# Finishing attention heads in pairs, with the softmax division moved behind the transpose, in a cached decode kernel

## The chip, the cores and the metric

The kernel runs on one core of one Trainium2 chip. The metric is the device time of one execution in microseconds (us). The engines are named PE (matmul), PEld (its weight loads), DVE (vector), ACT (scalar), POOL (GpSimd) and SP, which only issues loads here.

## The reference, cut to what matters

Two attention blocks A and B of the same shape are computed and their outputs put side by side. The batch is 2, with 32 heads of 192 in each block, one query, 8192 cached keys and values, and a model width of 640.

```python
q = (x @ wq).reshape(B, 1, 32, 192)
scores = einsum("bhqd,bhkd->bhqk", q, k_cache) * 192 ** -0.5
o = einsum("bhqk,bhkd->bhqd", softmax(scores), v_cache)
out = o.reshape(B, 1, 32 * 192) @ wo              # once for A, once for B
```

## The kernel before

One **unit** is one head of one batch row, so there are 128 units. A unit loads 3 MB of K and 3 MB of V (the cached keys and values), all issued by SP. Each engine's work is put by hand into a table of slots, and the engines then run their tables in order, held only by semaphores. The steps of unit `u` are:

1. DVE multiplies K by the query in two products. `d1a` takes the first `NA` of the 64 key columns, which ACT then sums. `d1b` takes the others, which DVE sums itself. The end of `d1b` frees the K buffer.
2. DVE takes the maximum (`d3`), and POOL reduces it over the partitions (`ar`). ACT takes the exponential, and POOL reduces its sum (`ls`).
3. PE forms P·V with 32 matmuls (`pv`), whose end frees the V buffer.
4. Per head (two units), ACT copies the result out of PSUM, where the matmuls accumulate (`f1`), and DVE forms the reciprocal of the sums (`f2`). PE transposes the result by a matmul against the reciprocals, which also divides (`f3`), ACT copies the transposed result (`f4`), and PE multiplies by `wo` (`f5`).

The tiles stand in memory in the order in which they are made. `ND_MAX` is what the two products' split leaves to DVE, and it sets the size of `prodD`:

```python
NA_MAX = max(NA_MAIN, NA_LAST)                     # 28 and 23: NA of all units, and of the last one
ND_MAX = T - min(NA_MAIN, NA_LAST)                 # 64 - 23 = 41
kb = [sb(f"kb{i}", [128, T, Dh], BF16) for i in range(NK)]
vb = [sb(f"vb{i}", [128, T, Dh], BF16) for i in range(NV)]
prodA = [sb(f"prodA{i}", [128, NA_MAX, Dh], BF16) for i in range(2)]
prodD = sb("prodD", [128, ND_MAX, Dh], BF16)
# ... sc, mp, mg, nb, pb, rs, qbc
wqs = [sb(f"wqs{i}", [128, DC, HG * Dh], BF16) for i in range(2)]
wos = [sb(f"wos{i}", [128, HG // 2, 3, D], BF16) for i in range(2)]
```

The parts of the schedule that the argument touches are these (`put(table, slot, order, work, waits, signal)`):

```python
put(dve_tab, u + 1, 0, dve_d3(u), [("acc", u), ("r", u), key("ar", u - 2)], ("d3", u))
put(dve_tab, u, 2, dve_d1a(u), [("k", u), ("a0", qg_of(u)), key("acc", u - 2)], ("d1a", u))
put(dve_tab, u, 3, dve_d1b(u), ...)
# ...
early = (g == TAILG)                               # TAILG = G - 2, the next-to-last head
put(dve_tab, u1 + 2, 1 if early else 8, dve_f2(g), [("ls", u1), key("f3", g - 2)], ("f2", g))
```

Of the kernel before, what the change touches and what calls it, by code (L numbers as in the profile page):

```python
# [51 lines left out]
def build_kernel(nc, blocks, out, cfg=None):  # L52
# [11 lines left out]
    scale = float(Dh) ** -0.5  # L64

    NA_MAIN = min(cfg.get("NA", 28), T - 2)
    NA_LAST = min(cfg.get("NA_LAST", 23), T - 2)
    WARM = cfg.get("WARM", 3)
    NK = cfg.get("NK", 2)
    NV = cfg.get("NV", 2)  # L70
    HG = cfg.get("HG", 4)
# [24 lines left out]
    with ExitStack() as es:  # L96
# [16 lines left out]
        wos = [sb(f"wos{i}", [128, HG // 2, 3, D], BF16) for i in range(2)]  # L113
        xT = [[sb(f"xT{k}_{b}", [128, DC], BF16) for b in range(B)] for k in range(NBLK)]
        xbc = [[sb(f"xbc{k}_{b}", [128, DC, 128], BF16) for b in range(B)] for k in range(NBLK)]
        o_sb = sb("o_sb", [33, 2, Dh], F32)
        lall = [sb(f"lall{i}", [128, 2], F32) for i in range(2)]
        rc = [sb(f"rc{i}", [33, 2], F32) for i in range(2)]
        oTz = sb("oTz", [128, 3, 6], BF16)
        out_sb = [sb(f"out_sb{k}", [4, NH2], BF16) for k in range(NBLK)]  # L120
        actd = sb("actd", [128, 2], F32)

        qps = ps("qps", [128, 512], F32)
        ops = ps("ops", [128, 2, 512], F32)
        oTps = ps("oTps", [128, 512], F32)
        outps = ps("outps", [128, 512], F32)

# [19 lines left out]
        def key(name, *idx):  # L147
            for i in idx:
                if i < 0:
                    return None  # L150
            return (name,) + tuple(idx)
# [52 lines left out]
        def sp_wo(w):  # L204
            blk = (w * HG) // Hn
            h0 = (w * HG) % Hn
            src = blocks[blk]["wo"][h0 * Dh:(h0 + HG) * Dh, :].rearrange("(pr p i) n -> p pr (i n)", p=128, i=3)
            return dma(wos[w % 2][:].rearrange("p pr i n -> p pr (i n)"), src, wosem[w % 2])
# [50 lines left out]
            return lambda eng: eng.tensor_reduce(sc[u % 2][:, na:T], prodD[:, 0:T - na, 0:24], AXL.X, ALU.add)  # L259

        def dve_f2(g):
            return lambda eng: eng.reciprocal(rc[g % 2][:], lall[g % 2][0:33, :])

        def act_acc(u, t):
            return lambda eng: eng.activation(prodA[u % 2][:, t, :], prodA[u % 2][:, t, :], ACTF.Identity,  # L265
# [6 lines left out]
            return lambda eng: eng.activation(pb[u % 2][:, :, ::32], sc[u % 2][:].rearrange("p (j a) -> p j a", a=2),  # L272
                                              ACTF.Exp, bias=nb[u % 2][:], scale=scale, accum_out=rs[u % 2][:])

        def act_f1(eng):
            eng.activation(o_sb[0:1, :, :], ops[0:1, :, 0:Dh], ACTF.Identity)  # L276
            return eng.activation(o_sb[32:33, :, :], ops[32:33, :, Dh:2 * Dh], ACTF.Identity)  # L277

        def act_f1b(b):
            def fn(eng):  # L280
                eng.activation(o_sb[0:1, b, :], ops[0:1, b, 0:Dh], ACTF.Identity)
                return eng.activation(o_sb[32:33, b, :], ops[32:33, b, Dh:2 * Dh], ACTF.Identity)
            return fn

        def pe_warm(n, uu):
            vw = vb[uu % NV][:].rearrange("p (j a) d -> p j (a d)", a=2)

            def fn(eng):
                for i in range(n):
                    ins = eng.matmul(dps[0:33, 0:QW], pb[uu % 2][:, i % (T // 2), :], vw[:, i % (T // 2), :],  # L290
                                     start=(i == 0), stop=(i == n - 1))
                return ins
            return fn

        def act_f4(g):
            s0 = 64 * (g % 2)
            return lambda eng: eng.activation(oTz[s0:s0 + 64, :, 2:4],
                                              oTps[s0:s0 + 64, 0:6].rearrange("p (i b) -> p i b", i=3), ACTF.Identity)

        def act_a0(qg):  # L300
            return lambda eng: eng.activation(qbc[qg % 4][:], qps[:, 0:QW].rearrange("p (a d) -> p a d", a=2),  # L301
# [2 lines left out]
        def act_out(blk):  # L304
            return lambda eng: eng.activation(out_sb[blk][:], outps[0:4, 0:NH2], ACTF.Identity)  # L305
# [22 lines left out]
        def pe_pv(u, j0, j1):  # L328
            b = u % B
            vv = vb[u % NV][:].rearrange("p (j a) d -> p j (a d)", a=2)  # L330

            def fn(eng):
                for j in range(j0, j1):
                    ins = eng.matmul(ops[0:33, b, 0:QW], pb[u % 2][:, j, :], vv[:, j, :],  # L334
                                     start=(j == 0), stop=(j == T // 2 - 1))
                return ins
            return fn

        def pe_f3(g):
            s0 = 64 * (g % 2)  # L340

            def fn(eng):
                for i in range(3):
                    for b in range(B):
                        ins = eng.matmul(oTps[s0:s0 + 64, 2 * i + b:2 * i + b + 1],  # L345
                                         o_sb[:, b, :].rearrange("p (r i) -> p i r", i=3)[:, i, :],
                                         rc[g % 2][:, b:b + 1], start=True, stop=True)
                return ins
            return fn

        def pe_f5(g):
            first = (g % Hn == 0)
            last = (g % Hn == Hn - 1)
            w = g // HG
            pr = (g % HG) // 2
            s0 = 64 * (g % 2)

            def fn(eng):
                for i in range(3):
                    for half in range(2):  # L360
                        ins = eng.matmul(outps[0:4, 0:NH2], oTz[s0:s0 + 64, i, 2 - 2 * half:6 - 2 * half],  # L361
                                         wos[w % 2][s0:s0 + 64, pr, i, half * NH2:(half + 1) * NH2],
                                         start=(first and i == 0 and half == 0),
                                         stop=(last and i == 2 and half == 1))
                return ins
            return fn

        NSLOT = NU + 8
        TAILG = G - 2 if G >= 3 else -1

        dve_tab = [[] for _ in range(NSLOT)]
        act_tab = [[] for _ in range(NSLOT)]
# [3 lines left out]
        def put(tab, slot, order, fn, waits, sig):  # L376
            tab[slot].append((order, len(tab[slot]), fn, waits, sig))

        for u in range(NU):
# [14 lines left out]
                w = [("d1a", u), key("d3", u - 2), key("exp", u - 2)] if t == 0 else []  # L394
                put(act_tab, u, 10 + t, act_acc(u, t), w, ("acc", u) if t == na_of(u) - 1 else None)
            pc = pieces(u)
            w0 = [("exp", u), key("f1", g - 1), ("init",)]
            if pc is None:
                put(pe_tab, u, 0, pe_pv(u, 0, T // 2), w0 + [("v", u)], ("pv", u))
            else:  # L400
                for i, (t0, t1, sm) in enumerate(pc):
                    put(pe_tab, u, 0, pe_pv(u, t0 // 2, t1 // 2), (w0 if i == 0 else []) + [("vp", u, i)],
                        ("pv", u) if i == len(pc) - 1 else None)

        for g in range(G):
            u1 = 2 * g + 1
            early = (g == TAILG)
            if g == G - 1 and G >= 3:
                put(act_tab, u1 + 1, 3, act_f1b(0), [("pv", u1 - 1), key("f3", g - 1), ("init",)], ("f1a", g))
                put(act_tab, u1 + 2, 2, act_f1b(1), [("pv", u1), ("f1a", g)], ("f1", g))  # L410
            else:
                put(act_tab, u1 + 2, 2, act_f1, [("pv", u1), key("f3", g - 1), ("init",)], ("f1", g))
            put(dve_tab, u1 + 2, 1 if early else 8, dve_f2(g), [("ls", u1), key("f3", g - 2)], ("f2", g))
            put(pe_tab, u1 + 1 if early else u1 + 2, 3 if early else 1, pe_f3(g),
                [("f2", g), ("f1", g), key("f4", g - 1)], ("f3", g))
            put(act_tab, u1 + 3 if early else u1 + 4, 2 if early else 3, act_f4(g),
                [("f3", g), key("f5", g - 2), ("init",)], ("f4", g))
            w = [("f4", g), ("wo", g // HG)]
            if g % Hn == 0 and g > 0:
                w.append(("oev", g // Hn - 1))  # L420
            put(pe_tab, u1 + 3, 2, pe_f5(g), w, ("f5", g))
            if g == G - 1 and G >= 3 and WARM:
                put(pe_tab, u1 + 2, 1.5, pe_warm(WARM, NU - 1), [], ("warm", 1))
            if g % Hn == Hn - 1:
                blk = g // Hn
                put(act_tab, u1 + 5, 95, act_out(blk), [("f5", g)], ("oev", blk))
                put(act_tab, u1 + 5, 96, act_out_dma(blk, 0), [("oev", blk)], None)
                put(act_tab, u1 + 5, 97, act_out_dma(blk, 1), [("oev", blk)], None)

# [25 lines left out]
        for kind, u in korder:  # L455
            if kind == "k":
                if u in KSPLIT:
                    S_sp.add(sp_k(u, 0), waits=[key("d1b", u - NK)])
                    S_sp.add(sp_k(u, 1))
                else:  # L460
                    S_sp.add(sp_k(u), waits=[key("d1b", u - NK)])
                if u == 0:
                    if WQSPLIT:
                        S_sp.add(sp_wq(0, 1))
                    for blk in range(1, NBLK):
                        for b in range(B):
                            S_sp.add(sp_x(blk, b))
                w = u // UG
                if u % UG == 1:
                    S_sp.add(sp_wo(w), waits=[key("f5", (w - 2) * HG + HG - 1)])  # L470
                if u % UG == (3 if UG >= 8 else 0) and w + 1 < NWG:
                    S_sp.add(sp_wq(w + 1), waits=[key("pq", (w - 1) * HG + HG - 1)])
            else:
                add_v(u)

        S_pool.add(lambda eng: eng.memset(o_sb[:], 0.0))
        for i in range(2):
            S_pool.add((lambda i: (lambda eng: eng.memset(pb[i][:], 0.0)))(i))
        S_pool.add(lambda eng: eng.memset(oTz[:], 0.0), sig=("init",))
        for blk in range(1, NBLK):  # L480
            for b in range(B):
                S_pool.add(xbc_copy(blk, b), waits=[("x", blk)], sig=("xbc", blk) if b == B - 1 else None)
# [80 lines left out]
```

## Time and profile before

| | before |
|---|---|
| time, median of 4 runs | 2016.54 us (2011.67 to 2017.82) |
| DMA engines busy with the main queue | 98.6% |
| DVE, ACT, PE busy | 74%, 71%, 57% |
| last whole K load (unit 126) landed | 1971.72 us |
| last V load (unit 127) landed | 2001.81 us |
| end of the span | 2014.77 us |

The page of the kernel before, cut to its head and the parts on slices, queues and the chain of waits. In the second part each position is a fortieth of the span, and the GB/s row gives what the DMA engines moved in it:

```profile
span 2014.8 us, 20972 instructions
PE 1144.6 (57%) x5571; PEld 606.8 (30%) x5571; DVE 1482.1 (74%) x962; ACT 1436.9 (71%) x7805; POOL 113.0 (6%) x266
...
DMA  9999999999999999999999999999999999999995
GB/s 386 428 427 428 430 426 428 428 428 429 426 426 426 423 410 424 418 424 415 423 425 410 428 413 419 430 405 430 414 421 426 408 422 417 420 427 416 425 420 212
...
q1 hardware_dynamic: 55856, 836.79, 98.6%
q8 instruction: 44, 0.72, 0.1%
...
DMA 77%; DVE 21%; PE 1%; ACT 1%; POOL 0%; issue 0%; SPq 0%
```

The loads fill the span. The chain is K loads and the DVE products that free their buffers, and PE, ACT and POOL have next to no part in it. The waits say the same of PE. The columns are who waited, for what, us in total, times and the longest:

```profile
PE ops L334 <- DMA vb<-in_A_v_cache_dram: 442.9, 64, 23.0
PE ops L334 <- DMA vb<-in_B_v_cache_dram: 412.2, 62, 9.8
```

PE waits for V in 126 of 128 units. The chain of waits has no load in it after the K load of unit 126, the last that is loaded whole (unit 127's comes in two parts). From there on compute sets the pace, so this tail is shown closely. Here are DVE and then POOL of the kernel before, in order of time. The columns are start, duration in us, engine, line, operation, tiles, and in brackets the idle time before it and what ended that:

```profile
1984.56 0.22 DVE L251 TENSOR_REDUCE mp<-sc 128x1 f32<-128x64 f32 x1 [1.37 <-ACT prodA L265]
1984.69 0.15 DVE L262 RECIPROCAL rc<-lall 33x2 f32<-33x2 f32 x1
1984.77 2.43 DVE L244 TENSOR_TENSOR prodA<-kb,qbc 128x4416 bf16<-128x4416 bf16 x1
1987.12 4.24 DVE L248 TENSOR_TENSOR prodD<-kb,qbc 128x7872 bf16<-128x7872 bf16 x1
...
1984.87 6.71 POOL L231 PARTITION_ALL_REDUCE mg<-mp  x1 [13.07 <-DVE rc L262]
```

The reduction over partitions needs 0.35 us elsewhere in this trace (0.352 to 0.354 us in the other 127 units). Here it took 6.71 us, until both products were done, and ACT waited 7.09 us for it.

### The profile page before, as it was taken

Reading aid. Unit: us, or ns where it says so; the run is one execution under the profiler, and the core shown is the slowest. Engines: PE = TensorE matmul, PEld = TensorE weight load, DVE = VectorE, ACT = ScalarE, POOL = GpSimd, SP = SyncE. Lnnn points to the kernel's source line nnn. Section 1 sums busy time; section 2 is a strip of 40 time slices with the busy share of each in tenths; the row PEclk is TensorE's granted clock in tenths of the full one; section 3 lists DMA queues with packets and bytes.
Section 4 is the critical chain, followed back from the end, with each engine's and each line's share of the span. In section 5 each row is a group of like instructions: output and inputs, shape, how many; then the busy total and the mean of one; then the engine's idle time right before and its main releaser. Section 6 shows DMA issues by size and latency. Waiting matters only on the chain.

```text
span 2014.8 us, 20972 instructions
## 1 busy us (share of the span) xinstructions
PE 1144.6 (57%) x5571; PEld 606.8 (30%) x5571; DVE 1482.1 (74%) x962; ACT 1436.9 (71%) x7805; POOL 113.0 (6%) x266
## 2 busy tenths in 40 slices
PE   2565556556555565555655566555655565556557
PEld 1232233223232233223322333223322233223323
DVE  7776877867677777777777767777677767877775
ACT  6776777767767676776777767767677776777675
POOL 1000000000000001000000000000000000000001
PEclk9777777777777777777777777777777777777777
DMA  9999999999999999999999999999999999999995
GB/s 386 428 427 428 430 426 428 428 428 429 426 426 426 423 410 424 418 424 415 423 425 410 428 413 419 430 405 430 414 421 426 408 422 417 420 427 416 425 420 212
DMA packets 55991, 838.13 MB, mean 416 GB/s; under 512 B 7352, under 2 KB 18240, under 8 KB 22848
## 3 DMA queue, kind: packets, MB, share of 16 engines
q1 hardware_dynamic: 55856, 836.79, 98.6%
q8 instruction: 44, 0.72, 0.1%
q14 instruction: 75, 0.61, 0.1%
q10 hardware_dynamic: 16, 0.01, 0.0%
HBM read 836.77 MB, written 0.01 MB: 415 GB/s over the span
## 4 chain that ended last, share of the span: by engine, by line
DMA 77%; DVE 21%; PE 1%; ACT 1%; POOL 0%; issue 0%; SPq 0%
DMA kb<-in_B_k_cache_dram 39%; DMA kb<-in_A_k_cache_dram 38%; DVE prodD L248 12%; DVE prodA L244 9%; PE ops L334 1%; ACT prodA L265 0%; POOL mg L231 0%; PE outps L361 0%; PE oTps L345 0%; SPq L184 0%; SPq L191 0%; PE dps L290 0%; ACT o_sb L277 0%; ACT pb L272 0%; ACT out_sb L305 0%
## 5 line engine op out<-in xcount | busy, mean ns | idle before, releaser
L334 PE MATMUL ops<-vb,pb 128*33 128x384 bf16 x4096 | 952.7, 408 | 861.1 <-DMA vb<-in_A_v_cache_dram 442.9
L265 ACT ACTIVATE prodA<-prodA 128x192 bf16<-128x192 bf16 x3579 | 1238.5, 350 | 205.3 <-DVE prodA L244 204.6
L334 PEld LDWEIGHTS ops<-vb,pb 128*33 128x33 bf16 x4096 | 481.8, 120 | 1321.0 <-issue 1171.7
L265 ACT ACTIVATION_READ_ACCUMULATOR prodA<-prodA 128x1 f32 x3579 | 677.4, 189 | 0.0
L244 DVE TENSOR_TENSOR prodA<-kb,qbc 128x5376 bf16<-128x5376 bf16 x128 | 378.2, 2954 | 316.6 <-DMA kb<-in_A_k_cache_dram 160.2
L248 DVE TENSOR_TENSOR prodD<-kb,qbc 128x6912 bf16<-128x6912 bf16 x128 | 480.7, 3756 | 1.2 <-DMA kb<-in_A_k_cache_dram 1.2
L255 DVE TENSOR_TENSOR prodD<-prodD 128x3456 bf16<-128x3456 bf16 (+2 forms) x384 | 465.0, 1211 | 13.3
L251 DVE TENSOR_REDUCE mp<-sc 128x1 f32<-128x64 f32 x128 | 28.2, 220 | 180.0 <-ACT prodA L265 179.9
L231 POOL PARTITION_ALL_REDUCE mg<-mp x128 | 51.4, 402 | 1773.7 <-DVE mp L251 1760.7
L259 DVE TENSOR_REDUCE sc<-prodD 128x36 f32<-128x864 bf16 x128 | 134.9, 1054 | 4.4
L276 ACT ACTIVATE o_sb<-ops 1x384 f32<-1x384 f32 x63 | 30.3, 480 | 129.1 <-PE oTps L345 127.7
L301 ACT ACTIVATE qbc<-qps 128x384 bf16<-128x384 f32 x64 | 31.5, 492 | 125.4 <-PE qps L322 124.6
L269 ACT ACTIVATE nb<-mg 128x1 f32<-128x1 f32 x128 | 26.0, 203 | 100.8 <-POOL mg L231 100.8
L345 PEld LDWEIGHTS oTps<-rc,o_sb 33*64 33x64 f32 x768 | 72.0, 171 | 20.2 <-issue 20.2
L345 PE MATMUL oTps<-rc,o_sb 33*64 33x1 f32 x768 | 77.5, 225 | 0.0
L322 PE MATMUL qps<-wqs,xbc 128*128 128x384 bf16 x320 | 64.7, 334 | 6.7 <-DMA wqs<-in_A_wq_dram 6.1
L361 PE MATMUL outps<-wos,oTz 64*4 64x320 bf16 x384 | 62.3, 296 | 0.0
L235 POOL PARTITION_ALL_REDUCE lall<-rs x128 | 54.9, 429 | 103.0 <-ACT pb L272 103.0
L272 ACT ACTIVATE pb<-sc,nb 128x64 bf16<-128x64 f32 x128 | 52.2, 408 | 4.3
L361 PEld LDWEIGHTS outps<-wos,oTz 64*4 64x4 bf16 x384 | 26.3, 81 | 34.2 <-issue 16.2
L322 PEld LDWEIGHTS qps<-wqs,xbc 128*128 128x128 bf16 x320 | 26.4, 99 | 29.8 <-issue 9.9
L277 ACT ACTIVATE o_sb<-ops 1x384 f32<-1x384 f32 x63 | 30.4, 482 | 0.7
(20 smaller groups left out, 57.5 us busy)
## 6 DMA issues: line engine op xcount, KB each, us to landing
vb<-in_A_v_cache_dram SPq DMA_DIRECT2D x64, 3072.0 KB, 23.0
kb<-in_A_k_cache_dram SPq DMA_DIRECT2D x63, 3072.0 KB, 23.9
kb<-in_B_k_cache_dram SPq DMA_DIRECT2D x63, 3072.0 KB, 23.7
vb<-in_B_v_cache_dram SPq DMA_DIRECT2D x62, 3072.0 KB, 23.3
wos<-in_A_wo_dram SPq DMA_DIRECT2D x8, 960.0 KB, 25.2
wqs<-in_B_wq_dram SPq DMA_DIRECT2D x8, 960.0 KB, 27.9
wos<-in_B_wo_dram SPq DMA_DIRECT2D x8, 960.0 KB, 25.2
wqs<-in_A_wq_dram SPq DMA_DIRECT2D x7, 960.0 KB, 27.8
```

Of the source, the lines that this page charges most:

```text
L231: return lambda eng: eng.partition_all_reduce(mg[u % 2][:], mp[u % 2][:], 128, bass.bass_isa.ReduceOp.max)
L235: return lambda eng: eng.partition_all_reduce(lall[g % 2][:, b:b + 1], rs[u % 2][:], 128, bass.bass_isa.ReduceOp.add)
L244: return lambda eng: eng.tensor_tensor(prodA[u % 2][:, 0:na, :], kb[u % NK][:, 0:na, :], qb_bc(u, na), ALU.mult)
L248: return lambda eng: eng.tensor_tensor(prodD[:, 0:T - na, :], kb[u % NK][:, na:T, :], qb_bc(u, T - na), ALU.mult)
L255: return lambda eng: eng.tensor_tensor(prodD[:, 0:nd, 0:w], prodD[:, 0:nd, 0:w], prodD[:, 0:nd, w:2 * w], ALU.add)
L259: return lambda eng: eng.tensor_reduce(sc[u % 2][:, na:T], prodD[:, 0:T - na, 0:24], AXL.X, ALU.add)
L265: return lambda eng: eng.activation(prodA[u % 2][:, t, :], prodA[u % 2][:, t, :], ACTF.Identity, accum_out=sc[u % 2][:, t:t + 1])
L272: return lambda eng: eng.activation(pb[u % 2][:, :, ::32], sc[u % 2][:].rearrange("p (j a) -> p j a", a=2), ACTF.Exp, bias=nb[u % 2][:], s ...
L322: ins = eng.matmul(qps[:, 0:QW], xbc[blk][b][:, c, :], wqs[w % 2][:, c, off:off + QW], start=(c == 0), stop=(c == DC - 1))
L334: ins = eng.matmul(ops[0:33, b, 0:QW], pb[u % 2][:, j, :], vv[:, j, :], start=(j == 0), stop=(j == T // 2 - 1))
L345: ins = eng.matmul(oTps[s0:s0 + 64, 2 * i + b:2 * i + b + 1], o_sb[:, b, :].rearrange("p (r i) -> p i r", i=3)[:, i, :], rc[g % 2][:, b:b ...
L361: ins = eng.matmul(outps[0:4, 0:NH2], oTz[s0:s0 + 64, i, 2 - 2 * half:6 - 2 * half], wos[w % 2][s0:s0 + 64, pr, i, half * NH2:(half + 1) * ...
```

## The change

Its intent is to do the steps `f3` to `f5` once per head pair at 128 partitions instead of once per head at 64. The division moves out of the transpose into the copy after it, where it is a per-partition scale. A second PSUM accumulator lets the next head's P·V start before the copy. The tail's two constants were tuned anew, and warm-up matmuls on zeros were put before unit 126. The diff, cut to its core:

```diff
-    NA_LAST = min(cfg.get("NA_LAST", 23), T - 2)
-    WARM = cfg.get("WARM", 3)
+    NA_LAST = min(cfg.get("NA_LAST", 26), T - 2)
+    WARM = cfg.get("WARM", 10)
...
-        ops = ps("ops", [128, 2, 512], F32)
+        ops = [ps(f"ops{i}", [128, 2, 512], F32) for i in range(2)]
...
-        def act_f4(g):
-            s0 = 64 * (g % 2)
-            return lambda eng: eng.activation(oTz[s0:s0 + 64, :, 2:4],
-                                              oTps[s0:s0 + 64, 0:6].rearrange("p (i b) -> p i b", i=3), ACTF.Identity)
+        def act_f4(pp):
+            def fn(eng):
+                for b in range(B):
+                    ins = eng.activation(oTz[pp % 2][:, :, 2 + b], oTps[:, b:6:2], ACTF.Identity,
+                                         scale=rcT[pp % 2][:, b:b + 1])
+                return ins
+            return fn
...
+        def pe_f3(eng):
+            for i in range(3):
+                for b in range(B):
+                    ins = eng.matmul(oTps[:, 2 * i + b:2 * i + b + 1],
+                                     o_sb[:, b, :, :].rearrange("p s (r i) -> p i (s r)", i=3)[:, i, :],
+                                     ones33[:], start=True, stop=True)
+            return ins
...
-            w0 = [("exp", u), key("f1", g - 1), ("init",)]
+            w0 = [("exp", u), key("f1", g - 2), ("init",)]
...
-            put(dve_tab, u1 + 2, 1 if early else 8, dve_f2(g), [("ls", u1), key("f3", g - 2)], ("f2", g))
+            put(dve_tab, u1 + 2, 8, dve_f2(g), [("ls", u1), key("f4", pp - 2)], ("f2", g))
...  (f3 to f5 per pair; in the last pair f3 is cut into two halves)
```

More of the change, by code (lines that the diff above doesn't have):

```diff
@@ L115, in build_kernel @@
         xbc = [[sb(f"xbc{k}_{b}", [128, DC, 128], BF16) for b in range(B)] for k in range(NBLK)]
-        o_sb = sb("o_sb", [33, 2, Dh], F32)
+        o_sb = sb("o_sb", [33, 2, 2, Dh], F32)
+        ones33 = sb("ones33", [33, 1], F32)
+        wdl = sb("wdl", [128, 33], BF16)
+        wdr = sb("wdr", [128, QW], BF16)
         lall = [sb(f"lall{i}", [128, 2], F32) for i in range(2)]
-        rc = [sb(f"rc{i}", [33, 2], F32) for i in range(2)]
-        oTz = sb("oTz", [128, 3, 6], BF16)
+        rcT = [sb(f"rcT{i}", [128, 2], F32) for i in range(2)]
+        oTz = [sb(f"oTz{i}", [128, 3, 6], BF16) for i in range(2)]
         out_sb = [sb(f"out_sb{k}", [4, NH2], BF16) for k in range(NBLK)]
@@ L261, in dve_f2 @@
         def dve_f2(g):
-            return lambda eng: eng.reciprocal(rc[g % 2][:], lall[g % 2][0:33, :])
+            s0 = 64 * (g % 2)
+            return lambda eng: eng.reciprocal(rcT[(g // 2) % 2][s0:s0 + 64, :], lall[g % 2][s0:s0 + 64, :])
         def act_acc(u, t):
@@ L273, in act_exp, with act_f1, act_f1b, fn @@
                                               ACTF.Exp, bias=nb[u % 2][:], scale=scale, accum_out=rs[u % 2][:])
-        def act_f1(eng):
-            eng.activation(o_sb[0:1, :, :], ops[0:1, :, 0:Dh], ACTF.Identity)
-            return eng.activation(o_sb[32:33, :, :], ops[32:33, :, Dh:2 * Dh], ACTF.Identity)
-        def act_f1b(b):
+        def act_f1(g):
+            hs = g % 2
             def fn(eng):
-                eng.activation(o_sb[0:1, b, :], ops[0:1, b, 0:Dh], ACTF.Identity)
-                return eng.activation(o_sb[32:33, b, :], ops[32:33, b, Dh:2 * Dh], ACTF.Identity)
+                eng.activation(o_sb[0:1, :, hs, :], ops[hs][0:1, :, 0:Dh], ACTF.Identity)
+                return eng.activation(o_sb[32:33, :, hs, :], ops[hs][32:33, :, Dh:2 * Dh], ACTF.Identity)
+            return fn
+        def act_f1b(g, b):
+            hs = g % 2
+            def fn(eng):
+                eng.activation(o_sb[0:1, b, hs, :], ops[hs][0:1, b, 0:Dh], ACTF.Identity)
+                return eng.activation(o_sb[32:33, b, hs, :], ops[hs][32:33, b, Dh:2 * Dh], ACTF.Identity)
             return fn
         def pe_warm(n, uu):
-            vw = vb[uu % NV][:].rearrange("p (j a) d -> p j (a d)", a=2)
             def fn(eng):
                 for i in range(n):
-                    ins = eng.matmul(dps[0:33, 0:QW], pb[uu % 2][:, i % (T // 2), :], vw[:, i % (T // 2), :],
-                                     start=(i == 0), stop=(i == n - 1))
-                return ins
-            return fn
-        def act_f4(g):
-            s0 = 64 * (g % 2)
-            return lambda eng: eng.activation(oTz[s0:s0 + 64, :, 2:4],
-                                              oTps[s0:s0 + 64, 0:6].rearrange("p (i b) -> p i b", i=3), ACTF.Identity)
+                    ins = eng.matmul(dps[0:33, 0:QW], wdl[:], wdr[:], start=(i == 0), stop=(i == n - 1))
+                return ins
+            return fn
+        def act_f4(pp):
+            def fn(eng):
+                for b in range(B):
+                    ins = eng.activation(oTz[pp % 2][:, :, 2 + b], oTps[:, b:6:2], ACTF.Identity,
+                                         scale=rcT[pp % 2][:, b:b + 1])
+                return ins
+            return fn
         def act_a0(qg):
@@ L333, in fn @@
                 for j in range(j0, j1):
-                    ins = eng.matmul(ops[0:33, b, 0:QW], pb[u % 2][:, j, :], vv[:, j, :],
+                    ins = eng.matmul(ops[(u // B) % 2][0:33, b, 0:QW], pb[u % 2][:, j, :], vv[:, j, :],
                                      start=(j == 0), stop=(j == T // 2 - 1))
@@ L337, in pe_pv, with pe_f3h @@
             return fn
-        def pe_f3(g):
-            s0 = 64 * (g % 2)
+        def pe_f3(eng):
[5 more added lines that the diff above has]
+            return ins
+        def pe_f3h(hs):
+            s0 = 64 * hs
             def fn(eng):
@@ L345, in fn, with pe_f5 @@
                         ins = eng.matmul(oTps[s0:s0 + 64, 2 * i + b:2 * i + b + 1],
-                                         o_sb[:, b, :].rearrange("p (r i) -> p i r", i=3)[:, i, :],
-                                         rc[g % 2][:, b:b + 1], start=True, stop=True)
-                return ins
-            return fn
-        def pe_f5(g):
-            first = (g % Hn == 0)
-            last = (g % Hn == Hn - 1)
-            w = g // HG
-            pr = (g % HG) // 2
-            s0 = 64 * (g % 2)
+                                         o_sb[:, b, hs, :].rearrange("p (r i) -> p i r", i=3)[:, i, :],
+                                         ones33[:], start=True, stop=True)
+                return ins
+            return fn
+        def pe_f5(pp):
+            g0 = 2 * pp
+            first = (g0 % Hn == 0)
+            last = (g0 % Hn == Hn - 2)
+            w = g0 // HG
+            pr = (g0 % HG) // 2
             def fn(eng):
@@ L360, in fn @@
                     for half in range(2):
-                        ins = eng.matmul(outps[0:4, 0:NH2], oTz[s0:s0 + 64, i, 2 - 2 * half:6 - 2 * half],
-                                         wos[w % 2][s0:s0 + 64, pr, i, half * NH2:(half + 1) * NH2],
+                        ins = eng.matmul(outps[0:4, 0:NH2], oTz[pp % 2][:, i, 2 - 2 * half:6 - 2 * half],
+                                         wos[w % 2][:, pr, i, half * NH2:(half + 1) * NH2],
                                          start=(first and i == 0 and half == 0),
@@ L368, in build_kernel @@
         NSLOT = NU + 8
-        TAILG = G - 2 if G >= 3 else -1
         dve_tab = [[] for _ in range(NSLOT)]
@@ L403, in build_kernel @@
                         ("pv", u) if i == len(pc) - 1 else None)
+        LASTP = G // 2 - 1 if G >= 4 else -99
         for g in range(G):
             u1 = 2 * g + 1
-            early = (g == TAILG)
-            if g == G - 1 and G >= 3:
-                put(act_tab, u1 + 1, 3, act_f1b(0), [("pv", u1 - 1), key("f3", g - 1), ("init",)], ("f1a", g))
-                put(act_tab, u1 + 2, 2, act_f1b(1), [("pv", u1), ("f1a", g)], ("f1", g))
-            else:
-                put(act_tab, u1 + 2, 2, act_f1, [("pv", u1), key("f3", g - 1), ("init",)], ("f1", g))
@@ L413, in build_kernel @@
-            put(dve_tab, u1 + 2, 1 if early else 8, dve_f2(g), [("ls", u1), key("f3", g - 2)], ("f2", g))
-            put(pe_tab, u1 + 1 if early else u1 + 2, 3 if early else 1, pe_f3(g),
-                [("f2", g), ("f1", g), key("f4", g - 1)], ("f3", g))
-            put(act_tab, u1 + 3 if early else u1 + 4, 2 if early else 3, act_f4(g),
-                [("f3", g), key("f5", g - 2), ("init",)], ("f4", g))
-            w = [("f4", g), ("wo", g // HG)]
-            if g % Hn == 0 and g > 0:
-                w.append(("oev", g // Hn - 1))
@@ L421, in build_kernel @@
-            put(pe_tab, u1 + 3, 2, pe_f5(g), w, ("f5", g))
-            if g == G - 1 and G >= 3 and WARM:
-                put(pe_tab, u1 + 2, 1.5, pe_warm(WARM, NU - 1), [], ("warm", 1))
-            if g % Hn == Hn - 1:
-                blk = g // Hn
-                put(act_tab, u1 + 5, 95, act_out(blk), [("f5", g)], ("oev", blk))
+            pp = g // 2
+            w1 = [key("f3", pp - 1), ("init",)]
+            if pp == LASTP and g % 2 == 0:
+                put(act_tab, u1 + 3, 2, act_f1(g), [("pv", u1)] + w1, ("f1", g))
+            elif pp == LASTP:
+                put(act_tab, u1 + 1, 3, act_f1b(g, 0), [("pv", u1 - 1)] + w1, ("f1a", g))
+                put(act_tab, u1 + 2, 2, act_f1b(g, 1), [("pv", u1), ("f1a", g)], ("f1", g))
+            else:
+                put(act_tab, u1 + 2, 2, act_f1(g), [("pv", u1)] + w1, ("f1", g))
@@ new lines, in build_kernel @@
+            put(dve_tab, u1 + 2, 8, dve_f2(g), [("ls", u1), key("f4", pp - 2)], ("f2", g))
+        for pp in range(G // 2):
+            g1 = 2 * pp + 1
+            u1 = 2 * g1 + 1
+            if pp == LASTP:
+                put(pe_tab, u1 + 1, 1, pe_f3h(0), [("f1", g1 - 1), key("f4", pp - 1), ("init",)], ("f3a", pp))
+                put(pe_tab, u1 + 2, 1, pe_f3h(1), [("f1", g1), ("f3a", pp)], ("f3", pp))
+            else:
+                put(pe_tab, u1 + 2, 1, pe_f3, [("f1", g1 - 1), ("f1", g1), key("f4", pp - 1), ("init",)], ("f3", pp))
+            put(act_tab, u1 + 5 if pp == LASTP - 1 else u1 + 4, 3.5 if pp == LASTP - 1 else 3, act_f4(pp),
+                [("f3", pp), ("f2", g1 - 1), ("f2", g1), key("f5", pp - 2), ("init",)], ("f4", pp))
+            w = [("f4", pp), ("wo", (2 * pp) // HG), key("f5", pp - 1)]
+            if (2 * pp) % Hn == 0 and pp > 0:
+                w.append(("oev", (2 * pp) // Hn - 1))
+            put(pe_tab, u1 + 6 if pp == LASTP - 1 else u1 + 3, 1.2 if pp == LASTP - 1 else 2, pe_f5(pp), w, ("f5", pp))
+            if pp == LASTP and WARM:
+                put(pe_tab, u1 - 1, -0.5, pe_warm(WARM, NU - 3), [("init",)], ("warm", 1))
+            if g1 % Hn == Hn - 1:
+                blk = g1 // Hn
+                put(act_tab, u1 + 5, 95, act_out(blk), [("f5", pp)], ("oev", blk))
@@ L469, in build_kernel @@
                 if u % UG == 1:
-                    S_sp.add(sp_wo(w), waits=[key("f5", (w - 2) * HG + HG - 1)])
+                    S_sp.add(sp_wo(w), waits=[key("f5", ((w - 2) * HG + HG - 1) // 2 if w >= 2 else -1)])
                 if u % UG == (3 if UG >= 8 else 0) and w + 1 < NWG:
@@ L476, in build_kernel @@
         S_pool.add(lambda eng: eng.memset(o_sb[:], 0.0))
+        S_pool.add(lambda eng: eng.memset(ones33[:], 1.0))
+        S_pool.add(lambda eng: eng.memset(wdl[:], 0.0))
+        S_pool.add(lambda eng: eng.memset(wdr[:], 0.0))
         for i in range(2):
             S_pool.add((lambda i: (lambda eng: eng.memset(pb[i][:], 0.0)))(i))
-        S_pool.add(lambda eng: eng.memset(oTz[:], 0.0), sig=("init",))
+        S_pool.add(lambda eng: eng.memset(oTz[0][:], 0.0))
+        S_pool.add(lambda eng: eng.memset(oTz[1][:], 0.0), sig=("init",))
         for blk in range(1, NBLK):
```

## The prediction

> **What bounds the kernel now.** DMA. The page shows 837 MB in 2014.8 us, the 16 DMA engines 98.6% busy with the main queue; PE is 57%, DVE 74%, ACT 71% busy. The chain of waits is 77% K-cache loads plus 21% DVE products that free the K buffers. PE waits for V loads 126 times (855 us); a load lands a median 23 us after issue, so the queue keeps about 1.5 units (15.5 us each) of backlog.
>
> **One DMA engine is late.** The landing increments of each load (16, one per engine) show 15 engines together and one behind: 0.4 us at the start, 4 us more every 12 units, then a constant 12.5 us with the others held back; the page's GB/s falls from about 428 to 418. The packet list has a PE instruction queue (q8): 44 packets of 16 KB, 1.01 us each, one per 46 us: 2.2%, the same as the lag's growth (4.1 us per 186 us). My reading, an inference: PE's instruction fetch shares that engine, and that engine's work sets the time.[...]
>
> **The loop.** Per head pair instead of per head, transposes (768 matmuls, 77.5 us busy) and output projections (384, 62.3 us) halve; the doubled output accumulator spares the next head's PV the wait for the eviction (about 1 us). All this compute is slack behind DMA, worth about nothing directly. But PE goes from 5571 matmuls to about 5014; with weight loads about 1110 fewer of 11290 instructions, 4 to 5 fetches of 1.01 us: estimate -4.5 us.
>
> **The tail** (last 30 us) is where compute counts:
> - The all-reduce at 1984.9 took 6.7 us rather than 0.35 because DVE products ran back to back. [...]Max-reduce, then product: the order stays, so does the stall.
> - PV 126 no longer waits for the 0.96 us eviction; warm-up matmuls before it may raise its clock (8.3 us cold, 5.4 warm). But the last unit's ACT sums (23 to 26, +1.0 us at 0.345) start about 1 us earlier, so the last exp still ends about 2002.8; PV 127 starts 0.6 us earlier than 2003.5.
> - After it, two half transposes (1.14 us each) in a row and one projection replace projection, transpose, projection: 4.2 us for 3.6.
> - Risk: if PV 126 runs warm, PE idles up to 5 us before PV 127, which may start cold (+2 to +3 us).
> In sum about +0.7 us (0 to +3).
>
> **Prediction:** 2016.5 - 4.5 + 0.7, about 2013 us, range 2008.5 to 2017.5. Faster by over 2%: 0.01; within 2%: 0.98; slower by over 2%: 0.01.
>
> **What would show it right or wrong.** PE instruction packets about 40 instead of 44; the last V load landing (2001.8) some 4 us earlier; late-engine lag still 12 to 13 us; DMA still 98 to 99%; the tail's first all-reduce still 6 to 7 us; last landing to end 13 to 15 us (13.0 before). If the last landing doesn't move, fetches aren't the pacer. If that all-reduce is short, or PV 127 cold, my tail is wrong. Run-to-run spread (2011.7 to 2017.8) is as large as the effect. A loss would need a new PE wait that delays V issues by over 10 us; I see none.

2016.5 - 4.5 + 0.7 = 2012.7, which it rounds to 2013 us.

## The result, and the profile after

The changed kernel takes 2007.4 us (median of 10 runs, 2005.23 to 2009.66), against 2016.27 us for the kernel before (15 runs, 2011.67 to 2017.97). The ratio is 0.9958, with a 95% interval of 0.9949 to 0.9966. Ratios here are the mean time of one kernel's runs over that of the other's in the same rounds, so they are not quite the ratios of the medians. This is clearly a gain of some 9 us. The time lies below the range that was predicted (2008.5 to 2017.5 us), and the gain is 9 us where 3.5 were forecast.

The page of the changed kernel, the same lines:

```profile
span 2005.7 us, 19822 instructions
PE 1121.5 (56%) x5014; PEld 593.3 (30%) x5014; DVE 1484.8 (74%) x962; ACT 1435.6 (72%) x7811; POOL 141.2 (7%) x270
...
GB/s 387 431 428 431 431 427 432 429 429 430 429 427 428 426 414 429 415 428 419 415 430 413 422 424 418 431 406 419 424 412 433 408 423 421 410 433 419 424 417 243
...
q1 hardware_dynamic: 55856, 836.79, 98.8%
q8 instruction: 39, 0.64, 0.1%
...
DMA 77%; DVE 21%; ACT 1%; PE 0%; issue 0%; POOL 0%; SPq 0%
```

The kernel is bound as before. PE lost 557 matmuls and five instruction fetches, but its waits for V grew (by 18 us) about as its work shrank (by 23 us):

```profile
PE ops L344 <- DMA vb<-in_A_v_cache_dram: 448.3, 64, 22.9
PE ops L344 <- DMA vb<-in_B_v_cache_dram: 425.2, 63, 11.0
```

The gain has two parts, and the landing of unit 126's K divides them. It landed at 1966.34 us instead of 1971.72, so 5.4 us were gained in the loop. From there to the end it took 39.34 us instead of 43.05, so 3.7 us were gained in the tail. In the loop the DMA engines simply moved more per us: GB/s in the first slices is 431, 428, 431, 431 against 428, 427, 428, 430. Summed over the trace, the packets of the main queue took 1982.2 us per engine instead of 1987.0. In the tail the long reduction shrank. DVE and then POOL of the changed kernel:

```profile
1979.17 0.22 DVE L254 TENSOR_REDUCE mp<-sc 128x1 f32<-128x64 f32 x1 [1.36 <-ACT prodA L269]
1979.30 2.75 DVE L247 TENSOR_TENSOR prodA<-kb,qbc 128x4992 bf16<-128x4992 bf16 x1
1981.97 3.95 DVE L251 TENSOR_TENSOR prodD<-kb,qbc 128x7296 bf16<-128x7296 bf16 x1
...
1979.48 2.79 POOL L234 PARTITION_ALL_REDUCE mg<-mp  x1 [13.18 <-DVE mp L254]
```

It now ends shortly after the first product (which ends at 1982.05) instead of after both: 2.79 us instead of 6.71. The reciprocal that stood before the product is gone from there.

### The profile page after: what moved, and what is told of

The parts are those of the page before. It is cut to its first block, busy times and chain, and to the rows that moved or that the text cites. A ratio compares the mean times of both kernels' runs of the same rounds, so it can differ in the third digit from the quotient of the medians.

```text
span 2005.7 us, 19822 instructions
## 1 busy us (share of the span) xinstructions
PE 1121.5 (56%) x5014; PEld 593.3 (30%) x5014; DVE 1484.8 (74%) x962; ACT 1435.6 (72%) x7811; POOL 141.2 (7%) x270
## 3 DMA queue, kind: packets, MB, share of 16 engines
q1 hardware_dynamic: 55856, 836.79, 98.8%
## 4 chain that ended last, share of the span: by engine, by line
DMA 77%; DVE 21%; ACT 1%; PE 0%; issue 0%; POOL 0%; SPq 0%
DMA kb<-in_B_k_cache_dram 39%; DMA kb<-in_A_k_cache_dram 38%; DVE prodD L251 12%; DVE prodA L247 9%; ACT prodA L269 1%; PE ops L344 0%; POOL mg L234 0%; PE oTps L363 0%; PE outps L379 0%; SPq L187 0%; SPq L194 0%; ACT pb L276 0%; DVE mp L254 0%; ACT out_sb L315 0%; ACT nb L273 0%
## 5 line engine op out<-in xcount | busy, mean ns | idle before, releaser
L238 POOL PARTITION_ALL_REDUCE lall<-rs x128 | 86.0, 672 | 103.0 <-ACT pb L276 103.0
L352 PEld LDWEIGHTS oTps<-ones,o_sb 33*128 33x128 f32 x372 | 67.1, 257 | 9.8 <-issue 9.8
L352 PE MATMUL oTps<-ones,o_sb 33*128 33x1 f32 x372 | 69.8, 311 | 0.0
L379 PE MATMUL outps<-wos,oTz 128*4 128x320 bf16 x192 | 31.3, 299 | 0.1
L276 ACT ACTIVATION_READ_ACCUMULATOR pb<-sc,nb 128x1 f32 x128 | 24.0, 187 | 0.0
```

The costliest lines, as they stand in the source:

```text
L238: return lambda eng: eng.partition_all_reduce(lall[g % 2][:, b:b + 1], rs[u % 2][:], 128, bass.bass_isa.ReduceOp.add)
L276: return lambda eng: eng.activation(pb[u % 2][:, :, ::32], sc[u % 2][:].rearrange("p (j a) -> p j a", a=2), ACTF.Exp, bias=nb[u % 2][:], s ...
L352: ins = eng.matmul(oTps[:, 2 * i + b:2 * i + b + 1], o_sb[:, b, :, :].rearrange("p s (r i) -> p i (s r)", i=3)[:, i, :], ones33[:], start= ...
```

## The experiments

Every experiment was timed in five rounds against the kernel before, and all gave correct results; b_kvalign and a_align512 have four times, the others five. The first table gives for each profiled run where the loop ended (the landing of unit 126's K), how long the tail took after it, and the median durations of two kinds of DMA packets that started between 40 and 520 us. A 24576-byte packet is one partition's share of a K or V load, and a 1536-byte packet is a row of `wq`. Landings and packets were read from the trace's own records.

```
kernel                          K 126 landed    to the end   K/V packet   wq packet   ratio to before
before                             1971.72         43.05       916 ns       67 ns
changed                            1966.34         39.34       913          65          0.9958
b_pewaits                          1970.78         40.96       915          67          0.9987
b_poolwaits                        1969.59         42.77       916          67          0.9993
a_pewaits                          1965.77         39.31       913          65          0.9955
b_recip_late                       1971.07         39.07       916          68          0.9981
b_shift128                         1964.40         42.91       913          65          0.9977
a_shift128                         1971.48         39.33       916          67          0.9997
a_recip_early                      1965.26         46.06       913          65          0.9999
b_shift_w                          1965.81         42.51       913          65          0.9979
a_kvalign                          1952.88         39.32       912          65          0.9923
b_kvalign                          1955.64         44.11       912          65          0.9913
a_align512                         1954.51         40.51       912          65          0.9910
```

The names begin with `b` for edits of the kernel before and with `a` for edits of the changed kernel. The loop's end falls into three groups that don't overlap: 1969.6 to 1971.7, 1964.4 to 1966.3, and 1952.9 to 1955.6. The experiments ran on three chips, and no group is of one chip alone. The packets' lengths sort the runs in nearly the same way. The share of the K and V packets at 912 ns, the floor in this window, sorts them best: 20 to 21%, 47 to 48%, and over 99%. (The expectations below quote packets of 64, 61, 909 and 906 ns, from a reading that these traces don't give. Only the differences of about 3 ns can be compared.)

### First: is it PE's instruction fetch?

The prediction said that PE's fetches share a DMA engine that sets the pace. Waits that are met at once lengthen an instruction stream and leave the work and its order as they were:

```diff
+        WAITED = (S_pool.sem, 1)                       # S_dve.sem in b_poolwaits
+        def idle_waits(n):
+            def fn(eng):
+                for _ in range(n):
+                    eng.wait_ge(*WAITED)
+            return fn
+        for u in range(NU - 2):
+            put(pe_tab, u, 0.5, idle_waits(40), [], None)   # pool_tab, order 5 in b_poolwaits; 18 in a_pewaits
```

> The kernel before, plus 20 PE wait instructions per unit that are met at once (40 calls, two to an instruction), none in the last two units: 2520 instructions, so 10 more PE fetch packets of 16 KB (54 instead of 44). Theory (PE's instruction fetch shares the DMA engine that sets the pace): about +10 us, 2026, and the last V load lands 10 us later. Rival (the late DMA engine is late for another reason, and fetches are hidden; the gain came from less PE work in the loop): within 1 us of before[...].

> The same 2520 already met waits on POOL's stream instead of PE's: the same bytes of instructions, but in the other fetch queue (q14, 8 KB packets of 0.31 us, about 20 more of them). Theory with PE's fetches alone on the late DMA engine: no change (within 1 us), the late engine's lag stays. Rival (any instruction fetch slows the late engine, all share it): +6 us or more.

> The changed kernel with about 1134 met waits put back on PE, so that its stream is as long as before (44 fetch packets instead of 39), its matmuls unchanged. Theory: it loses the fetch part of the gain, +5 us, to about 2012.4, and keeps the tail's part (about 4 us below before). Rival (the gain in the loop is from fewer matmuls or from the second accumulator): stays at 2007.4.

The dose arrived, as the queue line of b_pewaits shows:

```profile
q8 instruction: 54, 0.88, 0.2%
```

But nothing got slower. b_pewaits took 2013.75 us against 2015.62 (ratio 0.9987, 0.9974 to 0.9999), and unit 126's K landed at 1970.78, within the group of before. b_poolwaits took 2014.83 us (0.9993), with 95 packets instead of 75 in the other fetch queue. a_pewaits, the changed kernel with its 44 fetches back, kept the whole gain: 2007.04 us (0.9955). The fetch theory is refuted in both directions. These runs also show that the shorter stream is not the loop's gain by another road, such as issue time on PE. The prediction counted each fetch at its full 1.01 us; here ten more fetches cost nothing measurable.

In its tail b_pewaits is 2 us shorter than before. Its trace shows why: the second product had to wait 0.49 us for its K part, and in that hole the reduction got through (2.54 us). In the trace of before that part landed at 1987.00, only 0.12 us before the product began, so by these times a delay of little more than 0.12 us would open such a hole (an estimate). Whether the dose delayed it or chance did is not shown: all five runs of b_pewaits are at 2013.0 to 2014.3 us, and one was profiled.

### Second: the reduction in the tail

In b_recip_late the kernel before has one number changed, which moves one 0.15 us reciprocal behind the last unit's products. In a_recip_early the changed kernel has it put back:

```diff
-            put(dve_tab, u1 + 2, 1 if early else 8, dve_f2(g), ...)      # b_recip_late
+            put(dve_tab, u1 + 2, 8, dve_f2(g), ...)

-            put(dve_tab, u1 + 2, 8, dve_f2(g), ...)                      # a_recip_early
+            put(dve_tab, u1 + 2, 1 if g == G - 2 else 8, dve_f2(g), ...)
```

> The kernel before with only its next-to-last head's reciprocal moved to where the changed kernel has it, behind the last unit's products instead of between the max-reduce and the product. Theory (that reciprocal lets the product get ahead so that the tail's max all-reduce misses the gap between the two products): the all-reduce falls from 6.7 to about 2.8 us and the time by about 4 us, to 2012.3. Rival (the length of the products, 23 to 26 columns, or chance decides it): 6.7 us stays, no change.

> The changed kernel with the next-to-last head's reciprocal put back between the last max-reduce and the last product, as before. Theory (this reciprocal makes the tail's all-reduce miss the gap between the two products): the all-reduce goes from 2.8 to about 6.7 us and the time up by 3 to 4 us, to about 2011. Rival (the all-reduce is shorter for another reason in the changed kernel): 2.8 us and 2007.4 stay.

b_recip_late took 2012.19 us (0.9981, 0.9967 to 0.9994). The reduction took 2.48 us, and the tail 39.07 us instead of 43.05. DVE and then POOL of b_recip_late:

```profile
1983.90 0.22 DVE L251 TENSOR_REDUCE mp<-sc 128x1 f32<-128x64 f32 x1 [1.37 <-ACT prodA L265]
1984.04 2.45 DVE L244 TENSOR_TENSOR prodA<-kb,qbc 128x4416 bf16<-128x4416 bf16 x1
1986.41 4.25 DVE L248 TENSOR_TENSOR prodD<-kb,qbc 128x7872 bf16<-128x7872 bf16 x1
...
1984.22 2.48 POOL L231 PARTITION_ALL_REDUCE mg<-mp  x1 [13.10 <-DVE mp L251]
```

a_recip_early took 2013.53 us (0.9999, 0.9987 to 1.0012), and the reduction was long again. POOL and then PE of a_recip_early:

```profile
1978.41 6.71 POOL L234 PARTITION_ALL_REDUCE mg<-mp  x1 [13.07 <-DVE rcT L266]
...
1985.88 5.38 PE L344 MATMUL ops<-vb,pb 128*33 128x384 bf16 x32 [1.93 <-ACT pb L276]
1996.26 7.50 PE L344 MATMUL ops<-vb,pb 128*33 128x384 bf16 x32 [5.01 <-ACT pb L276]
```

So the reciprocal's place decides it where no hole opens as in b_pewaits: in either kernel, whether the last unit has 23 or 26 columns, and whatever else is in the kernel. How long the reduction takes goes with the products. In all six traces with the reciprocal in front and the second product starting unhindered after the first (before, b_poolwaits, b_shift128, b_shift_w, b_kvalign and a_recip_early), it went on until both products were done, 6.71 us. In the seven without the reciprocal (changed, a_pewaits, a_shift128, a_kvalign, a_align512, a_kv_bal and b_recip_late) it went on until the first was done, 2.48 to 2.79 us. The first product starts before the reduction, by 0.10 to 0.11 us with the reciprocal and by 0.18 us without. What holds the reduction up while a product runs was not shown, nor why it doesn't get in between the products in the first case.

a_recip_early lost more than the 3 to 4 us expected, 6.7 us of its tail. P·V of unit 126 took 5.38 us, PE then stood idle for 5.01 us, and unit 127's P·V ran its first half at half clock (granted 0.50 until 2000 us, 1.00 from 2001) and took 7.50 us. In the changed kernel the same step waits 1.40 us and takes 5.38 us, at a granted clock of 1.00. The retuned tail therefore pays only while the reduction is short.

### Third: where the tiles lie

With the fetches ruled out, the packet lengths were compared: at the median those of the changed kernel are 2 to 3 ns shorter. The built programs, which give each tile its address, show a difference that the diff doesn't mention. With `NA_LAST` at 26, `prodD` is 3 × 192 × 2 = 1152 bytes per partition smaller. All later tiles move down by that much, and 1152 is 4.5 × 256. The weight tiles lay 128 bytes past a multiple of 256, and now begin on one. (That 256 is the grain to look at was at this point an assumption; a_align512 below tests a coarser one.) K and V buffers stayed where they were, 128 past one.

```
offset within 256 bytes     K, V buffers   wq, wo tiles
before, a_shift128              128            128
changed, b_shift128, b_shift_w  128              0
a_kvalign, b_kvalign              0              0
```

The rival is that something in the change itself speeds the DMA up, such as less PE work. An unused tile of 128 bytes per partition, and nothing else, tells them apart:

```diff
         prodD = sb("prodD", [128, ND_MAX, Dh], BF16)
+        pad0 = sb("pad0", [128, 64], BF16)            # b_shift128, a_shift128; right before wqs in b_shift_w
```

> The kernel before with one unused tile of 128 bytes per partition behind the product tile, so that every later tile (the weight tiles among them) begins 128 bytes further on; in the changed kernel the smaller product tile moved them by 1152 bytes, to the same place within 256 bytes. Theory A (where the weight tiles lie within 256 bytes sets the length of their DMA packets): 1536-byte packets fall from 64 to 61 ns, and the time by at least 2 us; if the address also explains the K and V packets (912 to 909 ns) by 5 to 6 us, to 2010. Rival B (less work on PE in the loop lets the DMA write faster, or another part of the change): packets and time stay as before.

> The changed kernel with the same 128-byte tile, which puts its weight tiles where the kernel before has them within 256 bytes. Theory A: packets back to 64 and 912 ns, the loop's gain lost, 2007.4 rises by 5 to 6 us to about 2013, of which the tail's gain of 4 us against before remains. Rival B: stays at 2007.4, packets at 61 and 909 ns.

> The kernel before with the unused 128 bytes placed right before the weight tiles, so that only these and what follows move; score, probability and query tiles stay. If the place of the weight tiles makes the loop's gain: the same 5 us as with the pad behind the product tile, 24576-byte packets at 909 ns. If it is a tile in between that engines read and write: only the 1536-byte packets get shorter (61 ns), at most 2 us gained.

b_shift128 took 2009.17 us against 2013.82 (0.9977, 0.9964 to 0.9989): the kernel before with a pad has all of the loop's gain, and its packets are those of the changed kernel. The packet lines of their pages, before and then b_shift128:

```profile
DMA packets 55991, 838.13 MB, mean 416 GB/s; under 512 B 7352, under 2 KB 18240, under 8 KB 22848
DMA packets 55991, 838.13 MB, mean 418 GB/s; under 512 B 7352, under 2 KB 18240, under 8 KB 22848
```

a_shift128 has the changed kernel's work at the old addresses. Its packets are back at 916 and 67 ns, unit 126's K landed at 1971.48, and it took 2013.68 us (0.9997, 0.9985 to 1.001). Its profiled tail is as short as the changed kernel's (39.33 us), so by the traces some 4 us should have remained, but the timed runs don't show them. The kernel before was quicker than usual in those rounds (2011.58 to 2016.06). It may be that some of its executions had a short reduction by a hole as in b_pewaits, but they were not profiled, and this stays open. b_shift_w took 2010.62 us (0.9979, 0.9966 to 0.9991): moving only the weight tiles and the small tiles behind them is enough.

The loop's end agrees. It lies at 1969.6 to 1971.7 in all five kernels with the weights at 128, and at 1964.4 to 1966.3 in all five with the weights at 0 and K and V at 128, whatever their PE work.

The weight tiles' own packets got shorter: a 1536-byte packet went from 67 to 65 ns, and a 3840-byte one of `wo` from 152 to 149. They account for only part of the gain: their sum fell from 82.8 to 80.5 us per engine, 2.3 of the 4.8 us. Why a packet is longer when its target lies 128 bytes past a multiple of 256 was not shown, nor why K and V packets also got shorter (916 to 913 ns) when only the weight tiles moved.

### Fourth: the same for K and V

If the offset matters, the 837 MB of K, V and weights should gain most from it.

```diff
+        pad0 = sb("pad0", [128, 64], BF16)
         kb = [sb(f"kb{i}", [128, T, Dh], BF16) for i in range(NK)]
```

This one line is all of b_kvalign. a_kvalign has it too, and a second pad behind `prodD` so that the weights stay on a multiple of 256. a_align512 has 384 bytes in front of K and 128 behind `prodD`. Its expectation is wrong on one point: built again, the program has K and V on multiples of 512, but the weights 256 past one. In a_kvalign it is the other way round.

> The changed kernel with 128 unused bytes before the K buffers and 128 behind the product tile: K and V buffers move from 128 to 0 within 256 bytes, the weight tiles stay at 0. If the address within 256 bytes is what a packet's length depends on, the 24576-byte packets become shorter still, by about 3 ns (909 to 906), and the time falls by some 6 us, to 2001. If not, no change.

> The kernel before with the unused 128 bytes placed before the K buffers: everything moves by 128 bytes, K, V and weight tiles all begin at a multiple of 256 bytes. Nothing of the change is in it. If address alone is worth 5 us for the weights and some 10 us more for K and V: 15 us below before, about 2000, and so below the changed kernel (2007.4). The tail's long all-reduce (6.7 us) stays.

> The changed kernel with 384 unused bytes before the K buffers and 128 behind the product tile: K, V and weight tiles begin at multiples of 512 bytes, where the run that gave 1997.7 had multiples of 256. If 256 bytes is the grain that counts, the same as that run (ratio to before about 0.992, K and V packets at a median of 912 ns between 40 and 520 us). If a coarser grain counts, faster by some us more.

a_kvalign took 1997.7 us (0.9923, 0.991 to 0.9937), b_kvalign 1997.58 us (0.9913, 0.99 to 0.9927), and a_align512 1997.92 us (0.991, 0.9893 to 0.9926). The kernel before with one unused tile thus beats the changed kernel. The three cannot be told apart, so neither K and V nor the weights gained anything from 512 instead of 256. The pads move the product tiles too; no DMA writes these, but no run moved K and V alone. By the profiled tails (44.11 against 39.32 us) b_kvalign should be some 5 us slower than a_kvalign. The timed runs don't show it: the profiled run of b_kvalign (2001.55) is the slowest of its four, that of a_kvalign (1994.15) the fastest of its five. So the tail's part differs between executions more than one trace of each can show. The GB/s row of b_kvalign against those above:

```profile
GB/s 391 430 429 433 432 428 432 431 430 432 431 432 431 427 427 430 417 428 421 419 431 414 429 424 421 429 410 432 419 407 431 412 429 424 423 430 419 429 419 203
```

The size was underestimated in a_kvalign's expectation. The loop ended 13.5 us earlier than in the changed kernel (1952.88 against 1966.34), not 6, while the K and V packets' mean between 40 and 520 us fell from 915.9 to 913.2 ns. Over the some 2048 such packets of each DMA engine that is an estimate of 5.5 us. Over the whole trace the main queue's packets took 1972.8 us per engine instead of 1982.2, which is 9.4 us. The remaining 4 us are not accounted for.

### Fifth: relieving the late DMA engine, which failed

In every trace one of the 16 landing increments of a load comes, after the first third, about 12 us after the others, and they get no further ahead of it. In the trace of before its lag grows by 2.7 to 3.9 us per 12 units up to there, and is then 11.3 to 13.7 us against the median of the other 15. The lag goes with one of the 16 DMA engines: when the others have run out, from 1996 to 2001 us, the DMA share is 0.06 to 0.07, a sixteenth. If that were the last DMA engine, six K loads that leave it out would relieve it. That a load of 120 partitions leaves one engine out, and that this is the last one, was the assumption, and no run here shows it. By it the engine would be spared 48 packets of 0.91 us, 44 us, which is an estimate (6 loads of 128 packets, over 16 engines 8 each). The edit, on top of a_kvalign:

```diff
+        SPLIT = {u for u in range(NU - 1) if u % 21 == 10}
...
+                    eng.dma_start(kb[u % NK][0:120], src[0:120]).then_inc(ksem[u % NK], 16)
+                    return eng.dma_start(kb[u % NK][120:128], src[120:128]).then_inc(ksem[u % NK], 16)
```

> The changed kernel with K, V and weight tiles aligned as in the run that gave 1997.7, and in six of the 128 units the K load cut into one of 120 and one of 8 partitions[...]. If the late engine is the last one, [...]the lag no longer grows to 12 us, and the time falls by 20 to 35 us, to 1965 to 1978. If the late engine is another one: no gain, up to 5 us lost.

It took 2128.05 us (1.0553), outside both cases of its expectation. This is some 130 us more than a_kvalign (in other rounds), some 21 to 22 us for each of the six. Its GB/s row shows where:

```profile
GB/s 392 430 405 353 430 431 430 430 431 277 418 410 420 422 416 351 326 420 415 419 432 414 313 355 412 429 418 425 367 305 427 415 428 418 417 311 354 426 413 255
```

The split loads moved at about half rate: around the first one the stretch from 155 to 165 us has 202 and 221 GB/s, with the DMA engines still busy (a share of 0.95 and 1.02). The six split loads have 25 landing increments each, where a whole load has 16. After the first one a single increment came 6.6 us ahead of the others (190.5 against 197.1 us) while another still came late (203.4). If an engine was spared and the early increment is its own, it was not the late one. Which engine is late, and why, stays open; it is not PE's fetches (b_pewaits, a_pewaits).

## Why the prediction was right or wrong

- **What bounds the kernel: right.** DMA is 98.8% busy, the chain is 77% DMA and 21% DVE, and 557 fewer matmuls only lengthened PE's wait for V.
- **The loop's gain: wrong in its cause.** The step that failed is "that engine's work sets the time" with PE's fetches in it: "4 to 5 fetches of 1.01 us: estimate -4.5 us". The count was right (39 packets instead of 44), and the last V load landed 5.2 us earlier (1996.61), near the "some 4 us" that was to confirm it. But ten more fetches cost nothing (b_pewaits), and putting five back cost nothing (a_pewaits). What was taken as evidence, a lag that grows by 2.2% beside fetches that fill 2.2% of the time, was a coincidence of two numbers, and that -4.5 lies near the measured -5.4 us is luck. The term is 0, and in its place stand 5.4 us from the weight tiles' offset within 256 bytes (b_shift128 and b_shift_w give them, a_shift128 takes them away). The prediction never looked at the addresses, although the diff's `NA_LAST` feeds a tile's size.
- **The tail: wrong in its sign.** The step that failed is "Max-reduce, then product: the order stays, so does the stall". A 0.15 us reciprocal between the two does leave that place, and the stall went from 6.71 to 2.79 us (b_recip_late and a_recip_early show it both ways). The tail became 3.7 us shorter instead of "about +0.7 us".
- **The rest of the tail: about right for the case that was assumed.** With the stall kept (a_recip_early) the changed tail is 3.0 us longer than that of before (46.06 against 43.05). This is the upper end of "0 to +3", and 2.1 us of it are the risk that was named, a cold P·V 127 (7.50 us instead of 5.38). The steps between P·V 127 and the output copy grew from 3.58 to 5.22 us there, and to 4.54 us in the changed kernel, where 4.2 was predicted.
- **The sum.** Predicted were -4.5 + 0.7 = -3.8 us. The traces show -5.4 - 3.7 = -9.1 us.
- **The change's own idea** (pairs of heads, deferred division, second accumulator) is worth about nothing here, as the prediction said of the loop. A pad in the old kernel gives the loop's gain (0.9977) and one moved reciprocal the tail's (0.9981), and the product of the two ratios is 0.9958, that of the whole change. No run had both edits at once.

## What to carry to other kernels

In a kernel bound by loads, compare the addresses of the load targets before and after a change: an unrelated tile's size can move them, and here one unused 128-byte tile was worth twice the whole change (0.9913 against 0.9958). Try load targets on multiples of 256 bytes: here they paid 17.8 us over 128 past one (b_kvalign, 1997.58 us against 2015.4). Test a coincidence of two rates by a dose before building on it, and look at what else stands between a GpSimd reduction and the long vector operations around it: one reciprocal of 0.15 us made it 6.71 us instead of 2.48 here (before, b_recip_late).
